# A long convolution with a gated layer on one core: the seams between its stages, and the third stage's reads in rows of 128

## The chip, the cores and the metric

The kernel runs on one core of one Trainium2 chip, in F32. Its engines are TensorE (PE; PEld is its loading of weights), VectorE (DVE), ScalarE (ACT), GpSimd (POOL) and SyncE (SP), which here only issues DMAs. DMAs are issued from SP's queue and from ACT's. The time is that of the whole program on the device in microseconds (us), the median over several runs.

## The reference

`x`, `v` are [4, 12800, 128]; the filter has an order of 64. The first half is a long causal convolution done as a product of spectra:

```python
h_mlp = np.maximum(pos_emb @ w1, 0.0) @ w2
window = np.exp(-0.01 * pos)[:, None]
h_filt = h_mlp * window
u = x * v
L = 2 * S
Uf = np.fft.rfft(u, n=L, axis=1)
Hf = np.fft.rfft(h_filt, n=L, axis=0)
y = np.fft.irfft(Uf * Hf[None, :, :], n=L, axis=1)[:, :S, :]
return (x * y).astype(np.float32)
```

Its result goes through a gated layer (`xp` is `x` with four zero rows ahead, K = 5):

```python
for k in range(K):
    gate_pre += conv_w[k][None, None, :] * xp[:, k:k + S, :]
gate = 1.0 / (1.0 + np.exp(-gate_pre))
val = x @ w_val
return (gate * val @ w_out).astype(np.float32)
```

## The kernel before, in words

The sequence of 12800 is split as J x N1 x N2 = 2 x 100 x 64. The transform of length 25600 then becomes sums over N1 and over N2, each a matmul with a table of cosines and sines. B = 4 batches and D = 128 channels make 512 columns (`BD`). The work goes in three stages, with DRAM between them.

**Stage 1** goes over 64 columns n of N2 in pairs q that mirror each other. SP reads 1 MB of `xv`, DVE multiplies x by v (L312) and forms sums and differences (`mirrored`, L321), PE multiplies by the table `fold` (L334), ACT copies the result to `st` (L336), and SP stores it to the array `a_u` in DRAM, rows 0 to 95 and 96 to 99 apart (class `_Split`, L118). The filter's work (`filt`) runs in between. Of each n there are two stores of `st`; the program's last ones are named below. While the last columns run, SP already begins to read pair 0 of the next stage: `load_pair(0, NL)` takes the first NL = 24 of 32 q. The rest comes from a second `load_a` (two DMAs, L213), whose data need the last stores.

**Stage 2** goes over 50 pairs p of rows of N1 (`NP`). `load_pair` reads 1 MB of `a_u` (and weights each fourth pair). `spectrum` multiplies by the tables (PE L419) into `z_ps`, four PSUM banks; `times` multiplies by the filter's spectrum (DVE L425) into `va`, `vb`, `vc`, `vd`; POOL adds `vb` to `va` in two parts (L504, L506) and `vd` to 768 columns of `vc` (L505); DVE adds the last 256 (L491, L494), behind a tiny copy `gate` that waits for POOL. `inverse` (PE L435) multiplies back into `c_ps` (two buffers of two banks), ACT copies that to `c_sb` (L442; two tiles, one for a pair, each for both j), and ACT's queue stores each half to the array `c_y` in DRAM (L443). The inverse of pair p - 1 stands in round p; the last round does those of 48 and 49.

```python
c_y = dram.tile([J, N1, 2 * N2, B, D], F32, name="c_y")
```

A row of `c_y` has 128 x 2 KB = 256 KB.

**Stage 3** goes over 32 groups s (`y_order`), R = 4 columns of N2 of one j in each. A group needs, for both c, 4 x 512 columns of all 100 rows of `c_y[j]`. They lie in `ag`, whose memory (the filter's spectrum in stage 1 and 2) becomes six blocks; group s takes two, so three groups fit. Groups 0 to 2 (`FIRST`) are read into it in stage 2, rows 0 to 79 by a plan (`early`), the rest when the pairs are done; later groups by `load_rows`, in halves of 1024 columns split in 96 and 4 rows: 8 DMAs a group. `load_x` reads `xr` (800 KB).

For each of the 4 columns: `y_sum` (PE L596, eight rows in the trace for two columns) multiplies 100 rows by the table `inv` into `sd`; `y_copy` (ACT L603) copies it to `sd_sb`; `y_trans` (PE L610) transposes it into `tp` and ACT copies a part to `dif` (L612); `y_join` (DVE L620, L621; POOL L623) forms y and multiplies by x, into `ext` (`tail` for a last group). Then the layer: `tap` (ACT L635, DVE L638), `sigmoid` (ACT L642), `value` (PE L647), `gated` (DVE L652), `project` (PE L657), `finish` (ACT L665 and the output's DMA from ACT's queue, L668). `WARM` matmuls on tables stand ahead of the first sums (L682).

Each stage opens pools of SBUF and PSUM (`p1`, `ps1`, `p2`, `ps2`, `p3`, `ps3`) and closes them at its end, so the next stage's tiles lie on the same memory, and the first instruction to write a tile waits for all that used that place. The loaded pairs lie in a pool `ld` of six buffers, open through stages 1 and 2. Within a stage each engine takes its instructions in the order in which they are written (`manual_schedule`); a scheduler may move those of one stage past those of another that it is not bound to. Each engine runs its own list strictly in order, so an instruction that waits holds all behind it.

Of the kernel before, what the change touches and what calls it, by code (L numbers as in the profile page):

```python
# [9 lines left out]
F32 = mybir.dt.float32  # L10
# [111 lines left out]
def tile_longconv_gate(  # L122
# [28 lines left out]
    c_y = dram.tile([J, N1, 2 * N2, B, D], F32, name="c_y")  # L151
# [3 lines left out]
    inv = const.tile([N1, 2, N2], F32, name="inv")  # L155
# [19 lines left out]
    nc.scalar.dma_start(out=inv, in_=t_inv)  # L175
# [16 lines left out]
    blocks = [ag.rearrange("p k j e -> p (k j e)")[:N1, i * CR:(i + 1) * CR] for i in range(N1 * J * FO // CR)]  # L192
# [39 lines left out]
    with tc.tile_pool(name="p1", bufs=1) as p1, tc.tile_pool(name="ps1", bufs=1, space=PSUM) as ps1:  # L232
# [112 lines left out]
        with tc.manual_schedule():  # L345
# [42 lines left out]
            store(*last)  # L388


    with tc.tile_pool(name="p2", bufs=1) as p2, tc.tile_pool(name="ps2", bufs=1, space=PSUM) as ps2:
# [37 lines left out]
        def inverse(p, j, terms):  # L429
            wk = loaded[p][1]  # L430
            c_ps = ps2.tile([128, 2, BD], F32, name="c_ps", bufs=2)
# [6 lines left out]
            if j == 0:  # L438
                c_sb = p2.tile([128, 2, J, B, D], F32, name="c_sb", bufs=2)
                outs[p] = c_sb  # L440
            c_sb = outs[p]
            nc.scalar.copy(out=c_sb[:, :, j].rearrange("p h b d -> p h (b d)"), in_=c_ps)  # L442
            nc.scalar.dma_start(  # L443
                out=c_y[j, 2 * p:2 * p + 2].rearrange("h p b d -> p h (b d)"),
                in_=c_sb[:, :, j].rearrange("p h b d -> p h (b d)"))

        outs = {}
# [11 lines left out]
        with tc.manual_schedule():  # L459
            for p in range(-1, NP + 1):  # L460
                now, nxt, old = 0 <= p < NP, p + 1 < NP, 0 <= p - 1
                if p < 0:
                    load_a(loaded[0][0], 0, NL, N2 // 2)
                for q in range(AHEAD + 1) if p < 0 else (p + AHEAD,):
                    if q < NP and q not in loaded:
                        loaded[q] = load_pair(q)
                if p in early:
# [27 lines left out]
                if now:  # L495
                    vc = p2.tile([128, 2, B, D], F32, name="vc", bufs=3)
                    vd = p2.tile([128, 2, B, D], F32, name="vd", bufs=2)
                    times(vc, z1[0], h[:, 0, 0:2], 2)
# [5 lines left out]
                    nc.gpsimd.tensor_tensor(va[:, 0:2], va[:, 0:2], vb[:, 0:2], op=ALU.add)  # L504
                    nc.gpsimd.tensor_tensor(vcf, vcf, vdf, op=ALU.add)  # L505
# [4 lines left out]
                if old:  # L510
                    if p < NP:
                        inverse(p - 1, 0, ((0, oa[:, 0]), (1, oa[:, 1])))
                    if p == NP - 1:
                        inverse(p, 0, ((0, va[:, 0]), (1, va[:, 1])))
                        for c in range(2):
                            load_k(0, c, 96, N1)
                    inverse(p - 1, 1, ((0, oa[:, 2]), (1, oa[:, 3, 0:PB]), (0, oc[:, 0]), (1, oc[:, 1])))
            for s in range(1, FIRST):
                for c in range(2):
                    load_k(s, c, 80, N1)  # L520
# [9 lines left out]
    with tc.tile_pool(name="p3", bufs=1) as p3, tc.tile_pool(name="ps3", bufs=1, space=PSUM) as ps3:  # L530
# [8 lines left out]
        def load_x(s):  # L539
# [4 lines left out]
            xr = p3.tile([D, R * ROW], F32, name="xr", bufs=2)  # L544
# [225 lines left out]
```

## Time and profile before

| | us |
|---|---|
| runs | 1163.94, 1168.69, 1157.94; median 1163.94 |
| profiled execution | 1167.67 |
| its span | 1165.5 |
| stage 1 ends, stage 2's first matmul on a loaded pair | 362.46 |
| stage 2's last store of `c_y` issued | 756.76 |
| stage 3's first copy `sd_sb` | 765.33 |

The profiled execution has 2.17 us outside its span. The span's times run from its start. In a row of a timeline stand the start, the length, the engine (with a q, its queue of DMAs), the line, what it writes and reads, and in brackets for how long the engine had been idle and who ended that. `PEclk` in a table of stretches is the share of the full clock that PE was granted; the DMA share is how busy the core's 16 DMA engines were in the mean.

### The profile page before, as it was taken

To read this page: it belongs to the slowest core of one execution; us is meant where nothing else is said; L and a number is where in the kernel's file an instruction comes from. 1 tells how busy PE (TensorE), PEld (TensorE's weight loads), DVE (VectorE), ACT (ScalarE), POOL (GpSimd) and SP (SyncE) were. 2 spreads that over 40 slices of the span, in tenths; PEclk is the share of its full clock that TensorE was granted. 3 is DMA by queue.
4 is the path that set the end of the run, shared out by engine and by line. 5 is a ranking of instruction groups with operands and counts; after the bars stand their busy time and mean duration, and the time that the engine had idled before them with its cause. 6 is when DMAs were issued, how large, how long until landed. Compare 5 with 4: busy or idle time off the path is not lost.

```text
span 1165.5 us, 17562 instructions
## 1 busy us (share of the span) xinstructions
PE 1046.1 (90%) x6208; PEld 492.1 (42%) x6208; DVE 969.3 (83%) x1150; ACT 615.7 (53%) x1000; POOL 775.2 (67%) x393
## 2 busy tenths in 40 slices
PE   4899887887764999999999999979999999999986
PEld 2455543443321444444444444434444444444432
DVE  5675445798944899999999999629999999999996
ACT  1366555665641344444444444346676767677763
POOL 3354332323313888889888889737889898898880
PEclk9999999998995899999999999988999999999999
DMA  9999999999987588988888998558999999999932
GB/s 364 350 417 403 361 352 345 353 341 350 344 268 286 209 311 300 317 300 302 303 312 287 362 339 321 178 176 218 283 288 285 264 292 278 278 289 284 284 119 113
DMA packets 92888, 344.60 MB, mean 296 GB/s; under 512 B 9774, under 2 KB 19418, under 8 KB 77610
## 3 DMA queue, kind: packets, MB, share of 16 engines
q1 hardware_dynamic: 58824, 263.74, 69.1%
q10 hardware_dynamic: 33978, 79.74, 17.8%
q8 instruction: 51, 0.84, 0.3%
q14 instruction: 35, 0.29, 0.1%
HBM read 212.37 MB, written 131.07 MB: 295 GB/s over the span
## 4 chain that ended last, share of the span: by engine, by line
PE 58%; DMA 28%; ACT 6%; DVE 4%; issue 2%; SPq 1%; ACTq 0%; DVEq 0%
PE c_ps L435 21%; DMA a_u<-st 19%; PE sd L596 9%; PE z_ps L419 9%; DMA ld<-in_xv_dram 6%; PE o_ps L657 6%; PE v_ps L647 5%; PE tp L610 5%; PE c_ps L404 2%; DVE gt L638 2%; PE fp L334 2%; ACT gt L635 1%; ACT o_sb L665 1%; DMA c_y<-c_sb 1%; ACT sg L642 1%
## 5 line engine op out<-in xcount | busy, mean ns | idle before, releaser
L623 POOL TENSOR_TENSOR ext<-yr,xr 128x400 f32<-128x400 f32 x120 | 301.6, 2515 | 44.0 <-DVE yr L621 41.9
L322 POOL TENSOR_TENSOR eo<-eo 128x512 f32<-128x512 f32 x62 | 116.8, 1904 | 212.0 <-DVE eo L321 212.0
L334 PE MATMUL fp<-eo,fold 64*128 64x512 f32 x768 | 194.4, 640 | 54.5 <-ACT st L336 40.1
L638 DVE SCALAR_TENSOR_TENSOR gt<-ext,cw,gt 128x1600 f32<-128x1600 f32 x128 | 241.5, 1887 | 0.8 <-ACT gt L635 0.8
L442 ACT COPY c_sb<-c_ps 128x1024 f32<-128x1024 f32 x100 | 101.3, 1013 | 204.6 <-PE c_ps L435 196.5
L336 ACT COPY st<-fp 128x1024 f32<-128x1024 f32 x128 | 124.2, 1015 | 133.2 <-DMA a_u<-st 81.5
L435 PE MATMUL c_ps<-va,ld 64*128 64x512 f32 (+1 forms) x800 | 166.6, 556 | 0.1
L425 DVE TENSOR_TENSOR va<-z_ps,h_sb 128x2048 f32<-128x2048 f32 x50 | 114.3, 2286 | 38.7 <-DMA ld<-a_u 30.4
L504 POOL TENSOR_TENSOR va<-va,vb 128x1024 f32<-128x1024 f32 x50 | 118.4, 2367 | 40.0 <-DVE vb L425 40.0
L419 PE MATMUL z_ps<-ld 64*64 64x512 f32 x800 | 122.4, 621 | 18.2 <-DMA ld<-a_u 16.3
L334 PEld LDWEIGHTS fp<-eo,fold 64*128 64x128 f32 x768 | 74.8, 197 | 135.8 <-issue 76.4
L596 PE MATMUL sd<-ag,inv 100*64 100x512 f32 x512 | 128.7, 620 | 1.6 <-ACT sd_sb L603 1.0
L657 PE MATMUL o_ps<-gd,wout 128*128 128x400 f32 x256 | 112.4, 521 | 19.7 <-DVE gd L652 10.9
L435 PEld LDWEIGHTS c_ps<-va,ld 64*128 64x128 f32 x800 | 74.2, 189 | 113.7 <-issue 110.2
L506 POOL TENSOR_TENSOR va<-va,vb 128x1024 f32<-128x1024 f32 x50 | 118.3, 2367 | 0.0
L603 ACT COPY sd_sb<-sd 128x512 f32<-128x512 f32 x128 | 76.1, 595 | 76.8 <-PE sd L596 54.1
L425 DVE TENSOR_TENSOR vb<-z_ps,h_sb 128x2048 f32<-128x2048 f32 x50 | 114.0, 2280 | 0.0
L647 PE MATMUL v_ps<-ext,wval 128*128 128x400 f32 x256 | 107.1, 500 | 0.0
L435 PE MATMUL c_ps<-vc,ld 64*128 64x512 f32 x400 | 94.2, 589 | 0.0
L610 PEld LDWEIGHTS tp<-ident,sd_sb 128*128 128x128 f32 x512 | 60.1, 144 | 78.9 <-PE sd L596 47.9
L505 POOL TENSOR_TENSOR vc<-vc,vd 128x768 f32<-128x768 f32 x50 | 91.2, 1824 | 2.2 <-issue 0.3
L610 PE MATMUL tp<-ident,sd_sb 128*128 128x128 f32 x512 | 81.9, 286 | 5.4 <-ACT sd_sb L603 3.8
(84 smaller groups left out, 1452.1 us busy)
## 6 DMA issues: line engine op xcount, KB each, us to landing
ld<-in_xv_dram SPq DMA_DIRECT2D x64, 1024.0 KB
c_y<-c_sb ACTq DMA_DIRECT2D x100, 512.0 KB
ld<-a_u SPq DMA_DIRECT2D x49, 1024.0 KB
a_u<-st SPq DMA_DIRECT2D x64, 768.0 KB
ag<-c_y SPq DMA_DIRECT2D x116, 384.0 KB
out_dram<-o_sb ACTq DMA_DIRECT2D x32, 800.0 KB
xr<-in_xt_dram SPq DMA_DIRECT2D x31, 800.0 KB
ld<-in_tab_w_dram SPq DMA_DIRECT2D x12, 768.0 KB
```

What stands on the lines that cost most here:

```text
L334: nc.tensor.matmul(out=fp[:, h], lhsT=fold[r, w], rhs=eo[r, o, :, l], start=i == 0, stop=i == len(terms) - 1)
L336: nc.scalar.copy(out=st[:, o].rearrange("k j (h b) d -> k h j (b d)", h=2), in_=fp)
L419: nc.tensor.matmul(out=zs[c][half[h]], lhsT=wk[half[c], 0, half[h]], rhs=a2[half[c], h, j], start=True, stop=True)
L425: nc.vector.tensor_tensor(out, z.rearrange("p (b d) -> p b d", d=D).unsqueeze(1).to_broadcast([128, n, B, D]), h_sb.unsqueeze(2).to_broadc ...
L435: nc.tensor.matmul(out=c_ps[:, h, 0:n], lhsT=wk[half[h], 1 + c], rhs=vt[half[h]].rearrange("p b d -> p (b d)"), start=(i == 0), stop=(i == ...
L504: nc.gpsimd.tensor_tensor(va[:, 0:2], va[:, 0:2], vb[:, 0:2], op=ALU.add)
L596: nc.tensor.matmul(out=sd[c * N2:(c + 1) * N2], lhsT=inv[:, c], rhs=ct[c][:, r * B * D:(r + 1) * B * D], start=True, stop=True)
L610: nc.tensor.transpose(out=tp[:, b], in_=t[:, b], identity=ident)
L623: nc.gpsimd.tensor_tensor(e[:, r0 + r], yr, xr, op=ALU.mult)
L638: nc.vector.scalar_tensor_tensor(gt, rows(t, k), cw[:, k:k + 1], gt, op0=ALU.mult, op1=ALU.add)
L647: nc.tensor.matmul(out=v_ps, lhsT=wval, rhs=rows(t)[:, r * ROW:(r + 1) * ROW], start=True, stop=True)
L657: nc.tensor.matmul(out=o_ps, lhsT=wout, rhs=gd, start=True, stop=True)
```

## The change

- The two loads of pair 0's end are written behind the last store of stage 1, not at the head of stage 2.
- `c_sb` is one tile for each inverse ([128, 2, BD], five buffers), not one for a pair (two buffers of twice the size).
- In the last pair, DVE does the addition of `va[:, 0:2]` and that of 768 columns of `vc`; POOL keeps that of `va[:, 2:4]`.
- The rows 80 to 95 of groups 0 to 2 are read ahead of the last inverses, rows 96 to 99 of all three behind the inverse (49, 0). Before, groups 1 and 2 took rows 80 to 99 at the stage's end.
- PSUM of stage 2 is in two pools, `psz` (`z_ps`) and `psc` (`c_ps`). Stage 3's first tiles (`xr`, `sd_sb`, `dif`, `yr`, `tail`; in PSUM `sd` and `tp3`) have pools of their own, `y3` and `psy`, opened ahead of `p3` and `ps3`: they come to lie on `ld` and on `z_ps`.
- Two warm-up matmuls for four, into `tp3`.
- `c_y` has J x N1 = 200 rows in one dimension. `load_rows` reads 128 of them in one DMA for each c: rows 0 to 127 for j = 0, rows 72 to 199 for j = 1 (`EDGE` = 72). In j = 1 the 100 rows needed then stand 28 lower, and `y_sum` runs over 128 rows with a table that is zero in the first 28. That table takes the place of `fold` (of which `inv` is now a view) and is read in round 4 of stage 2 from SP, 128 KB, where before 50 KB came from ACT's queue at the start.

```diff
+            load_a(loaded[0][0], 0, NL, N2 // 2)
...
-            if j == 0:
-                c_sb = p2.tile([128, 2, J, B, D], F32, name="c_sb", bufs=2)
...
+            c_sb = p2.tile([128, 2, BD], F32, name="c_sb", bufs=5)
...
-                if p < 0:
-                    load_a(loaded[0][0], 0, NL, N2 // 2)
...
+                if p == 4:
+                    nc.sync.dma_start(out=inv, in_=t_inv)
...
+                    if not nxt:
+                        nc.vector.tensor_tensor(va[:, 0:2], va[:, 0:2], vb[:, 0:2], op=ALU.add)
                     times(vc, z1[0], h[:, 0, 0:2], 2)
                     times(vd, z1[1], h[:, 1, 0:2], 2)
...
+                    else:
+                        nc.vector.tensor_tensor(vcf, vcf, vdf, op=ALU.add)
...
-            for s in range(1, FIRST):
-                for c in range(2):
-                    load_k(s, c, 80, N1)
...
+    with tc.tile_pool(name="y3", bufs=1) as y3, tc.tile_pool(name="psy", bufs=1, space=PSUM) as psy, \
+            tc.tile_pool(name="p3", bufs=1) as p3, tc.tile_pool(name="ps3", bufs=1, space=PSUM) as ps3:
...
-                rows_ = c_y[j].rearrange("k p b d -> k p (b d)")
-                for h in range(0, R, R // 2):
-                    sync_s.dma_start(
-                        out=t[:, h * B * D:(h + R // 2) * B * D],
-                        in_=rows_[:, n0 + h:n0 + h + R // 2].rearrange("k p e -> k (p e)"))
+                nc.sync.dma_start(
+                    out=t, in_=c_y[j * EDGE:j * EDGE + 128, n0:n0 + R].rearrange("k p b d -> k (p b d)"))
...
-            sd = ps3.tile([128, B * D], F32, name="sd", bufs=2)
+            k = slice(0, N1 if s < NG else 128)
+            sd = psy.tile([128, B * D], F32, name="sd", bufs=2)
...
-                    out=sd[c * N2:(c + 1) * N2], lhsT=inv[:, c], rhs=ct[c][:, r * B * D:(r + 1) * B * D],
+                    out=sd[c * N2:(c + 1) * N2], lhsT=inv[k, s // NG, c], rhs=ct[c][k, r * B * D:(r + 1) * B * D],
...
-                w_ps = ps3.tile([D, 2 * D], F32, name="o_ps", bufs=2)
-                nc.tensor.matmul(
-                    out=w_ps, lhsT=ident, rhs=dft.rearrange("p a k -> p (a k)"), start=True, stop=True)
+                w_ps = psy.tile([D, B, 128], F32, name="tp3", bufs=2)
+                nc.tensor.matmul(out=w_ps[:, 0:2], lhsT=ident, rhs=dft, start=True, stop=True)
```

How instructions move is seen in three places. First, SP's list at the end of stage 1 (`a_u<-st` are stores, `ld<-a_u` the loads of pairs; here the last two stores and the loads for pairs 0 and 1), before:

```order
L118 DMA a_u<-st 96x2048
L118 DMA a_u<-st 4x2048
L213 DMA ld<-a_u 16x2x1024
L118 DMA a_u<-st 96x2048
L118 DMA a_u<-st 4x2048
L213 DMA ld<-a_u 16x2x1024
L227 DMA ld<-a_u 128x2x1024 x3
```

and after:

```order
L121 DMA a_u<-st 96x2048
L121 DMA a_u<-st 4x2048
L121 DMA a_u<-st 96x2048
L121 DMA a_u<-st 4x2048
L215 DMA ld<-a_u 16x2x1024 x2
L229 DMA ld<-a_u 128x2x1024 x3
```

The first of the two loads stood between the last two stores; now both stand behind them.

Second, PE's list at the end of stage 2, from the last inverse of an earlier pair on (`z_ps` is `spectrum`, `c_ps` are inverses, `o_ps` and `tp_...` from `dft` the warm-up matmuls, `sd` the first sums of stage 3), before:

```order
L419 MATMUL z_ps<-ld 64x512 x8
L435 MATMUL c_ps<-va,ld 128x512 x6
L435 MATMUL c_ps<-va,ld 128x256 x2
L435 MATMUL c_ps<-vc,ld 128x512 x4
L435 MATMUL c_ps<-va,ld 128x512 x10
L435 MATMUL c_ps<-va,ld 128x256 x2
L435 MATMUL c_ps<-vc,ld 128x512 x4
L435 MATMUL c_ps<-va,ld 128x512 x2
L435 MATMUL c_ps<-va,ld 128x256 x2
L435 MATMUL c_ps<-vc,ld 128x512 x4
L682 MATMUL o_ps<-dft,ident 128x256 x4
L596 MATMUL sd<-ag,inv 64x512 x4
```

and after:

```order
L423 MATMUL z_ps<-ld 64x512 x8
L439 MATMUL c_ps<-va,ld 128x512 x6
L439 MATMUL c_ps<-va,ld 128x256 x2
L439 MATMUL c_ps<-vc,ld 128x512 x4
L684 MATMUL tp_5505<-dft,ident 128x256
L684 MATMUL tp_5507<-dft,ident 128x256
L439 MATMUL c_ps<-va,ld 128x512 x10
L439 MATMUL c_ps<-va,ld 128x256 x2
L439 MATMUL c_ps<-vc,ld 128x512 x4
L439 MATMUL c_ps<-va,ld 128x512 x2
L439 MATMUL c_ps<-va,ld 128x256 x2
L439 MATMUL c_ps<-vc,ld 128x512 x4
```

The warm-up matmuls now stand ahead of the inverses of pairs 48 and 49, and the sums follow the last inverse directly. The banks of `tp` are those of `z_ps`.

Third, DVE's list at the same place (`va`, `vb`, `vc`, `vd` of pair 49 come from `z_ps` and the filter's spectrum `h_sb`; `gate` and the rows beside it belong to pair 48 or 49's inverse), before:

```order
L425 TENSOR_TENSOR va<-z_ps,h_sb_5264 128x2048
L425 TENSOR_TENSOR vb<-z_ps,h_sb_5264 128x2048
L491 TENSOR_TENSOR vc<-vc,vd 128x256
L493 COPY gate<-va 128x1
L494 TENSOR_TENSOR vc<-vc,va 128x256
L425 TENSOR_TENSOR vc<-z_ps,h_sb_5264 128x1024
L425 TENSOR_TENSOR vd<-z_ps,h_sb_5264 128x1024
```

and after:

```order
L429 TENSOR_TENSOR va<-z_ps,h_sb_5312 128x2048
L429 TENSOR_TENSOR vb<-z_ps,h_sb_5312 128x2048
L490 TENSOR_TENSOR vc<-vc,vd 128x256
L492 COPY gate<-va 128x1
L493 TENSOR_TENSOR vc<-vc,va 128x256
L498 TENSOR_TENSOR va<-va,vb 128x1024
L429 TENSOR_TENSOR vc<-z_ps,h_sb_5312 128x1024
L429 TENSOR_TENSOR vd<-z_ps,h_sb_5312 128x1024
L509 TENSOR_TENSOR vc<-vc,vd 128x768
```

The addition L498 stands ahead of the last two products that read `z_ps`, and L509 right behind them.

More of the change, by code (lines that the diff above doesn't have):

```diff
@@ L29 @@
 R = 4
-WARM = 4
+WARM = 2
 NC1 = N1 // 2 + 1
+EDGE = J * N1 - 128
 def _tables():
@@ L149, in tile_longconv_gate @@
     a_u = dram.tile([N1, 2, N2 // 2, 2, J, B, D], F32, name="a_u")
-    c_y = dram.tile([J, N1, 2 * N2, B, D], F32, name="c_y")
+    c_y = dram.tile([J * N1, 2 * N2, B, D], F32, name="c_y")
     fwd = const.tile([N1, 3, N1], F32, name="fwd")
     fold = const.tile([128, 3, 128], F32, name="fold")
-    inv = const.tile([N1, 2, N2], F32, name="inv")
+    inv = fold[:, 0:2].rearrange("p j (c n) -> p j c n", c=2)
     win = const.tile([N1, J, N2], F32, name="win")
@@ L191, in tile_longconv_gate @@
     CR = R * B * D
-    blocks = [ag.rearrange("p k j e -> p (k j e)")[:N1, i * CR:(i + 1) * CR] for i in range(N1 * J * FO // CR)]
+    blocks = [ag.rearrange("p k j e -> p (k j e)")[:, i * CR:(i + 1) * CR] for i in range(N1 * J * FO // CR)]
     y_order = [(j, g) for j in range(J) for g in [N2 // R - 1] + list(range(N2 // R - 1))]
@@ L202, in load_k @@
         nc.sync.dma_start(
-            out=block(s, c)[k0:k1], in_=c_y[j, k0:k1, n0:n0 + R].rearrange("k p b d -> k (p b d)"))
+            out=block(s, c)[k0:k1], in_=c_y[j * N1 + k0:j * N1 + k1, n0:n0 + R].rearrange("k p b d -> k (p b d)"))
     NP, PG = N1 // 2, KG // 2
@@ L388, in tile_longconv_gate @@
             store(*last)
-    with tc.tile_pool(name="p2", bufs=1) as p2, tc.tile_pool(name="ps2", bufs=1, space=PSUM) as ps2:
+            load_a(loaded[0][0], 0, NL, N2 // 2)
+    with tc.tile_pool(name="p2", bufs=1) as p2, tc.tile_pool(name="psz", bufs=1, space=PSUM) as psz, \
+            tc.tile_pool(name="psc", bufs=1, space=PSUM) as psc:
         BD = B * D
@@ L395, in bank @@
         def bank():
-            return ps2.tile([128, BD], F32, name="z_ps", bufs=4)
+            return psz.tile([128, BD], F32, name="z_ps", bufs=4)
         def filter_pair(p):
-            h_ps = ps2.tile([128, J, BD], F32, name="c_ps", bufs=2)[:, :, 0:2 * D].rearrange("p j (c d) -> p j c d", c=2)
+            h_ps = psc.tile([128, J, BD], F32, name="c_ps", bufs=2)[:, :, 0:2 * D].rearrange("p j (c d) -> p j c d", c=2)
             for c in range(2):
@@ L430, in inverse @@
             wk = loaded[p][1]
-            c_ps = ps2.tile([128, 2, BD], F32, name="c_ps", bufs=2)
+            c_ps = psc.tile([128, 2, BD], F32, name="c_ps", bufs=2)
             for i, (c, vt) in enumerate(terms):
@@ L437, in inverse @@
                         start=(i == 0), stop=(i == len(terms) - 1))
-            if j == 0:
-                c_sb = p2.tile([128, 2, J, B, D], F32, name="c_sb", bufs=2)
[L440 to L447, printed above, removed]
+            c_sb = p2.tile([128, 2, BD], F32, name="c_sb", bufs=5)
+            nc.scalar.copy(out=c_sb, in_=c_ps)
+            nc.scalar.dma_start(out=c_y[j * N1 + 2 * p:j * N1 + 2 * p + 2].rearrange("h p b d -> p h (b d)"), in_=c_sb)
         filt_p, z_p, v_p = {}, {}, {}
@@ L473, in tile_longconv_gate @@
                 if p == NP - 1:
-                    for c in range(2):
-                        load_k(0, c, 80, 96)
+                    for s in range(FIRST):
+                        for c in range(2):
+                            load_k(s, c, 80, 96)
                 if now:
@@ L514, in tile_longconv_gate @@
                         inverse(p, 0, ((0, va[:, 0]), (1, va[:, 1])))
[L515 to L516 removed]
+                        for s in range(FIRST):
+                            for c in range(2):
+                                load_k(s, c, 96, N1)
                     inverse(p - 1, 1, ((0, oa[:, 2]), (1, oa[:, 3, 0:PB]), (0, oc[:, 0]), (1, oc[:, 1])))
[L518 to L520 removed]
     ld_pool.__exit__(None, None, None)
[L530 removed]
+    with tc.tile_pool(name="y3", bufs=1) as y3, tc.tile_pool(name="psy", bufs=1, space=PSUM) as psy, \
+            tc.tile_pool(name="p3", bufs=1) as p3, tc.tile_pool(name="ps3", bufs=1, space=PSUM) as ps3:
         HALO = KC - 1
@@ L601, in y_copy @@
         def y_copy(s, r):
-            t = p3.tile([128, B, D], F32, name="sd_sb", bufs=3)
+            t = y3.tile([128, B, D], F32, name="sd_sb", bufs=3)
             nc.scalar.copy(out=t.rearrange("p b d -> p (b d)"), in_=sds.pop((s, r)))
```

23 lines of the change are left out of this document (12 added, 11 removed).

## The prediction

> **What bounds the kernel now.** I read the page first: the span and the share of each engine.
>
> ```profile
> span 1165.5 us, 17562 instructions
> PE 1046.1 (90%) x6208; PEld 492.1 (42%) x6208; DVE 969.3 (83%) x1150; ACT 615.7 (53%) x1000; POOL 775.2 (67%) x393
> ```
>
> TensorE (PE) is busy 90% of the span, so there are some 119 us in which it is not. The next view is the busy time by stretches, which shows where they lie.
>
> ```profile
> core 0: us, PE busy (x) PEld busy (x) DVE busy (x) ACT busy (x) POOL busy (x), PEclk, DMA share, GB/s
> 330.00:375.00 45.00, 23.53 (x150) 9.52 (x148) 14.41 (x11) 13.75 (x21) 5.73 (x3) 0.74 0.80 265
> 400.00:500.00 100.00, 100.00 (x738) 44.21 (x736) 98.54 (x92) 41.80 (x66) 90.34 (x53) 1.00 0.85 297
> 740.00:760.00 20.00, 18.21 (x88) 8.53 (x82) 8.04 (x10) 6.08 (x6) 11.11 (x6) 1.00 0.63 200
> 760.00:780.00 20.00, 16.16 (x68) 6.68 (x68) 3.87 (x13) 7.57 (x17) 6.17 (x6) 0.83 0.67 199
> 780.00:800.00 20.00, 17.25 (x72) 7.35 (x71) 15.57 (x21) 12.09 (x22) 12.82 (x8) 0.83 0.68 192
> 900.00:1000.00 100.00, 96.99 (x410) 44.54 (x409) 96.28 (x137) 72.45 (x128) 88.75 (x35) 1.00 0.94 280
> ```
>
> Stage 2 (400 to 500) and stage 3 (900 to 1000) leave PE nothing or 3%; in stage 3 VectorE (DVE) has as little room, and the DMA engines stand at 0.94. PE idles at the seams: 21 us from 330 to 375, some 8 from 740 to 800, and in both the granted clock drops. The change works on both seams and on stage 3's transfers, so there are three terms: A, B and C.
>
> **A: the first pair's end of load, put last in stage 1.** SyncE's (SP's) timeline, the chain of waits and PE's timeline at the first seam:
>
> ```profile
> 343.66 11.24 DMA a_u<-st
> 354.92 0.32 SPq L213 DMA_DIRECT2D ld<-a_u  x1
> 355.33 0.74 SPq L118 DMA_DIRECT2D a_u<-st  x2
> 359.60 0.32 SPq L213 DMA_DIRECT2D ld<-a_u  x1
> 362.46 3.54 PE L419 MATMUL z_ps<-ld 64*64 64x512 f32 x16 [16.29 <-DMA ld<-a_u]
> ```
>
> The first half of the load (L213) goes out at 354.92, when the last store but one has landed (343.66 + 11.24 = 354.90). The last store stands behind it on SP and goes at 355.33; the second half waits for that, goes at 359.60, and PE starts 2.86 us later. After the change both halves stand behind the last store, which then follows the other without the 10 us of waiting. If the two overlap, the last store lands soon after 354.9. From its own issue it needed 359.60 - 355.33 = 4.27 us, some of which is its bytes queued behind its predecessor's; I let it land 2 us after, at 357.0. The load goes then, 2.6 us earlier. Bounds: 0 (all 4.27 us follow the predecessor) and 4.3 (they vanish in its 11.24). PE is full from 400 on, so nothing is late behind it: **A = -2.6**.
>
> **B: the seam from stage 2 to 3.** The timelines of ScalarE (ACT), PE, and DVE:
>
> ```profile
> 751.25 1.01 ACT L442 COPY c_sb<-c_ps 128x1024 f32<-128x1024 f32 x1 [2.87 <-DMA c_y<-c_sb]
> 765.33 1.07 ACT L603 COPY sd_sb<-sd 128x512 f32<-128x512 f32 x2 [8.59 <-DMA c_y<-c_sb]
> ```
>
> ```profile
> 745.43 5.12 PE L435 MATMUL c_ps<-va,ld 64*128 64x512 f32 x24
> 753.77 1.91 PE L435 MATMUL c_ps<-vc,ld 64*128 64x512 f32 x8
> 756.79 1.99 PE L682 MATMUL o_ps<-dft,ident 128*128 128x256 f32 x8 [1.10 <-ACT c_sb L442]
> 759.33 2.79 PE L596 MATMUL sd<-ag,inv 100*64 100x512 f32 x8 [0.55 <-DMA ag<-c_y]
> 765.97 1.11 PE L610 MATMUL tp<-ident,sd_sb 128*128 128x128 f32 x4 [3.85 <-ACT sd_sb L603]
> 767.08 3.61 PE sd L596 x8
> ```
>
> ```profile
> 744.78 1.22 DVE L425 TENSOR_TENSOR vc<-z_ps,h_sb 128x1024 f32<-128x1024 f32 x1
> 745.91 1.22 DVE L425 TENSOR_TENSOR vd<-z_ps,h_sb 128x1024 f32<-128x1024 f32 x1
> L321 DVE TENSOR_TENSOR eo<-u,ld 128x1024 f32<-128x1024 f32 x64 | 76.9, 1240 | 4.8 <-PE fp L334 0.9
> ```
>
> Stage 3's first copy waits 8.59 us, to 765.33, for the last c_y store: its tile lies on memory that the store still reads. With pools of their own the copy waits for the sums and its PSUM bank only. That would be worth all of 765.33 - 759 less a sum, were PE not delayed first. It is: the order shows the two warm-up matmuls ahead of the last two pairs' inverses, in `psy`, on the banks that DVE's last `vd` reads. In before `vd` ends at 745.91 + 1.22 = 747.13. Ahead of it now stands an addition of 1024 columns that GpSimd (POOL) did; the nearest row is L321's, 1.24 us. So `vd` ends at 748.3. PE, which in before began its next matmuls at 745.43, waits 2.9 us with the four inverses queued behind. Then two warm-ups (half of 1.99): 749.3. The inverses took from 745.43 to 753.77 + 1.91 = 755.68, 10.25 us: they end at 759.5. Pair 49's first store follows the second inverse, at about a third of the four's 10.25 us, so 752.8, and its copy of 1.01: it goes at 753.9, where before it went at 752.3 (the copy of 751.25 was that one). Its landing and the small read of its rows bring the sums some 1.6 us later than before's 759.33 less the two warm-ups' time saved: I take 759.6, and 760.6 for the first copy. Gain 4.7 us.
>
> Behind the copy, before's sums ran slowly: 3.61 us for eight, against 1.87 in the rows below, a stretch at half clock. If it goes, 2.8 us more are won (1.74 on these eight, the rest on the transposes and sums beside them): B = -7.5. If PE's new wait of 2.9 us brings a throttled stretch of its own, as waits do between 760 and 800 (clock 0.83 with PE busy 81 to 86%, hence 0.17 x 20 = 3.4 us lost in each), little of the 2.8 stays and up to 2.7 more go: -2. I take **B = -6.0**, nearer to the first.
>
> [...]
>
> **C: stage 3's reads of c_y.** The chain of waits gives the period of a step (8 steps from the first of these rows to the last), SP's timeline the issue, the page the sizes:
>
> ```profile
> 804.75 1.87 PE sd L596 x8
> 862.35 1.87 PE sd L596 x8
> 897.30 1.87 PE sd L596 x8
> 842.42 5.19 SPq L118 DMA_DIRECT2D ag<-c_y  x8
> ag<-c_y SPq DMA_DIRECT2D x116, 384.0 KB
> ag<-c_y SPq DMA_DIRECT2D x116, 16.0 KB
> xr<-in_xt_dram SPq DMA_DIRECT2D x31, 800.0 KB
> out_dram<-o_sb ACTq DMA_DIRECT2D x32, 800.0 KB
> ```
>
> A step takes (897.30 - 804.75) / 8 = 11.57 us. It reads 4 x (384 + 16) = 1600 KB of c_y in 29 steps. Now it reads 2 x 1024 = 2048 KB, 28% more, in 2 DMAs for 8. The price hangs on the rate; these answers show the transfers while one kind runs nearly alone: c_y in rows of 8 KB (628, 714.9), in 4 KB (787.5), `xr` (768), the output (852).
>
> ```profile
> DMA packets 61, 0.50 MB, mean 250 GB/s; under 512 B 0, under 2 KB 0, under 8 KB 0
> DMA packets 54, 0.43 MB, mean 266 GB/s; under 512 B 2, under 2 KB 2, under 8 KB 2
> DMA packets 318, 1.09 MB, mean 242 GB/s; under 512 B 54, under 2 KB 54, under 8 KB 316
> DMA packets 150, 0.86 MB, mean 429 GB/s; under 512 B 16, under 2 KB 16, under 8 KB 150
> DMA packets 110, 0.59 MB, mean 397 GB/s; under 512 B 12, under 2 KB 12, under 8 KB 110
> ```
>
> c_y comes at 242 to 266 GB/s, `xr` and the output at 429 and 397. Transfers of one step: `xr` 0.819 / 0.429 = 1.91, output 0.819 / 0.397 = 2.06, c_y 2.097 MB at 258 (the middle of the 8 KB rows) 8.13: 12.1 us. Against 11.57 the DMA engines become the bound, by 0.53 x 29 = 15.4 us; from this goes what the buffers hold: a read issued at 842.42 is used at 862.35, 19.9 us later, and needs about one period, so 8.6 are slack. That leaves 6.8. [...] Bounds: at 266 GB/s 11.85 us, 8.1 us in all, within the slack, so 0; at 242 it is 12.64, 31 - 8.6 = +22.
>
> [...]
>
> **At nothing**, with what covers it: the fold table's 128 KB read in pair 4 on SP (ACT loses a read at the start; stage 2 has a DMA share of 0.85); K = 128 in place of 100 (a matmul's time goes with its columns: 620 ns at K = 100 and 621 at 64 in the groups); five `c_sb` (ACT is busy 41.8 of 100, only the wait of 2.87 at the seam counts, and it is in B); last-pair additions (POOL has less to do, DVE's 1.2 us are in B). The groups for K:
>
> ```profile
> L596 PE MATMUL sd<-ag,inv 100*64 100x512 f32 x512 | 128.7, 620 | 1.6 <-ACT sd_sb L603 1.0
> L419 PE MATMUL z_ps<-ld 64*64 64x512 f32 x800 | 122.4, 621 | 18.2 <-DMA ld<-a_u 16.3
> ```
>
> Sum: -2.6 - 6.0 + 4 = -4.6. The profiled execution took 1167.67 (2.2 outside its span), 3.7 over the median 1163.94; taken off the median: **1159**.
>
> **Rivals.** First, slower: stage 3 becomes bound by its transfers. From 0.6 us over the period on, thus below 256 GB/s, C eats A and B; at 242, +22 gives 1163.94 + 13.4 = 1177, at 250 (12.36 us, +14.3) 1170. For it speak the DMA share of 0.94 before a byte is added, and the slowest of the c_y rows; against it that PE there never waits for a read. [...] Second, B is lost: warm-ups ahead of the inverses, PE waiting behind `vd`, a slow clock behind that. B = -2, in all -0.6: 1163. Third, all gains: whole rows over all partitions reach 266 or more, the clock stays up, A lies between its middle and its bound: -10.1 to -11.8, so 1152 to 1154. Fourth, the load's new place does nothing, since the last store's bytes follow the other's anyway: A = 0, 1162; it lies within the others.
>
> **Chances.** Forecast 0.45 (A and B as worked out, C from 0 to 9: 1155 to 1164), slow reads 0.25, B lost 0.1, all gains 0.2. A measurement of this kernel can't tell less than 1% (11.6 us) from no change. Faster by more than that, under 1152.3, is the better half of all gains, 0.1, and 0.08 that I add to either side for what no row shows: 0.18. Slower, over 1175.6, needs C of 20, reads at 244 or less: half of the slow reads, 0.12, and the same 0.08: 0.2. The rest, 0.62, lies within. The range goes from the better end of all gains with the unknown's first part, 1148, to slow reads at 242, 1177.
>
> **What would show it.** A: the load on SP issued at about 357 and PE's first `z_ps` at 359.9. B: a gap of PE of 2.9 us ahead of the warm-ups, released by DVE's `vd`; the first `sd_sb` copy right behind the first sums, with no wait for a c_y store; the clock between 760 and 800 at 0.9 or above. C: stage 3's period, 11.57 or longer, PE's sums waiting for `ag` or not, the DMA share near 1.0 and over 300 GB/s. The prediction is wrong if the sums wait for reads by more than 18 us in all, or if stage 1 or 2 takes another time between its seams.

## The result, and the profile after

| | before | changed |
|---|---|---|
| median, first comparison (9 runs each) | 1163.94 | 1155.03 |
| ratio, with its 95% interval | | 0.9917 (0.9891 to 0.9944) |
| median, second comparison (33 and 12 runs) | 1163.31 | 1157.37 |
| ratio, with its 95% interval | | 0.9948 (0.9919 to 0.9976) |
| span of the profiled execution | 1165.5 | 1155.8 |

The change makes the kernel faster by some 6 to 9 us, under 1%; both intervals lie below 1. The forecast was 1159, with "within 1%" as the likeliest case. A ratio is estimated by itself and differs a little from the quotient of the medians (1155.03 / 1163.94 would be 0.9923). Three executions fell in a slower state, one of before (beside the first four variants), one of the changed kernel with the old reads and the profiled one of the run that reads rows 80 to 91 earlier, so the medians below leave them out and that profile's times aren't compared.

The page of the changed kernel begins so, and its table of stretches (the columns are those of before's) follows.

```profile
span 1155.8 us, 17291 instructions
PE 1045.2 (90%) x6204; PEld 488.4 (42%) x6204; DVE 963.2 (83%) x1152; ACT 616.3 (53%) x1000; POOL 775.2 (67%) x391
```

```profile
330.00:375.00 45.00, 28.51 (x156) 9.77 (x156) 19.88 (x17) 10.43 (x18) 14.07 (x9) 0.68 0.80 270
740.00:760.00 20.00, 17.62 (x60) 6.72 (x59) 0.56 (x3) 4.75 (x6) 0.00 (x0) 0.76 0.74 152
760.00:780.00 20.00, 18.24 (x92) 7.75 (x91) 8.00 (x22) 12.48 (x27) 10.22 (x10) 0.94 0.68 249
780.00:800.00 20.00, 17.65 (x75) 8.38 (x74) 20.00 (x29) 12.41 (x20) 18.18 (x7) 0.91 0.67 257
900.00:1000.00 100.00, 97.00 (x412) 44.40 (x408) 96.29 (x137) 72.16 (x125) 88.56 (x35) 1.00 0.81 314
```

PE's busy time is the same to 1 us, so what was won is waiting. Two things stand out. The clock is now lower than before between 740 and 760 (0.76 against 1.00), ahead of the place where it was low, and higher behind it (0.94 and 0.91 from 760 to 800, against 0.83 twice). And stage 3 (900 to 1000) moves 314 GB/s against 280, more as its reads are longer, with a *smaller* share of DMA time: 0.81 against 0.94.

The first seam, in the chain of waits, SP's timeline and PE's timeline:

```profile
338.70 11.51 DMA a_u<-st
348.13 2.47 SPq L215 DMA_DIRECT2D ld<-a_u  x2
353.01 3.46 PE L423 MATMUL z_ps<-ld 64*64 64x512 f32 x16 [13.17 <-DMA ld<-a_u]
```

The last store goes at 338.70, when its copy is done, and not 10 us later. The load's two halves wait for the last two stores: the first goes at 348.13, when the last store but one has landed, the second at 350.3, when the last has (338.70 + 11.51 = 350.21). So the last store lands 2.1 us after the other.

The second seam, in DVE's, PE's and ACT's timelines and the chain of waits:

```profile
737.56 1.21 DVE L429 TENSOR_TENSOR vd<-z_ps,h_sb 128x1024 f32<-128x1024 f32 x1
738.92 2.04 PE L684 MATMUL tp<-dft,ident 128*128 128x256 f32 x4 [2.82 <-DVE vd L429]
740.89 7.12 PE L439 MATMUL c_ps<-va,ld 64*128 64x512 f32 x24
753.52 1.04 PE L598 MATMUL sd<-ag,fold 100*64 100x512 f32 x2 [0.79 <-DMA ag<-c_y]
756.16 3.68 PE L598 MATMUL sd<-ag,fold 100*64 100x512 f32 x6 [1.60 <-DMA ag<-c_y]
758.17 0.58 ACT L605 COPY sd_sb<-sd 128x512 f32<-128x512 f32 x1 [4.37 <-PE sd L598]
```

```profile
747.82 2.96 DMA c_y<-c_sb
751.13 4.99 DMA ag<-c_y
```

The copy into `sd_sb` no longer waits for a store. The hoisted warm-ups wait 2.82 us for DVE's `vd`. Behind them 24 matmuls of the inverses take 7.12 us, where 24 took 5.12 in before: the granted clock is 0.50 from 738.39 to 745.22. Pair 49's store goes at 747.82. The first two of the eight rows of sums run at 753.52; the other six need another read of rows 96 to 99, which goes at 751.13 and takes 4.99 us.

Stage 3, by the chain of waits and by the transfers from 791 to 794, where c_y is read almost alone:

```profile
794.87 1.87 PE sd L598 x8
887.42 1.87 PE sd L598 x8
DMA packets 171, 1.27 MB, mean 423 GB/s; under 512 B 16, under 2 KB 16, under 8 KB 16
```

Between the same two groups as in before lie (887.42 - 794.87) / 8 = 11.57 us a step, unchanged. The reads run at 423 GB/s, where before's ran at 242 to 268.

### The profile page after: what moved, and what is told of

It reads as the page before. It is cut to its first block, busy times and chain, and to the rows that moved or that the text cites. A ratio compares the mean times of both kernels' runs of the same rounds, so it can differ in the third digit from the quotient of the medians.

```text
span 1155.8 us, 17291 instructions
## 1 busy us (share of the span) xinstructions
PE 1045.2 (90%) x6204; PEld 488.4 (42%) x6204; DVE 963.2 (83%) x1152; ACT 616.3 (53%) x1000; POOL 775.2 (67%) x391
## 4 chain that ended last, share of the span: by engine, by line
PE 59%; DMA 25%; DVE 7%; ACT 6%; issue 2%; ACTq 0%; POOL 0%; SPq 0%; DVEq 0%
PE c_ps L439 20%; DMA a_u<-st 13%; PE sd L598 9%; DMA ld<-in_xv_dram 9%; PE z_ps L423 9%; PE o_ps L659 6%; PE v_ps L649 5%; PE tp L612 5%; PE fp L336 2%; PE c_ps L408 2%; DVE gt L640 2%; DMA ld<-in_pos_dram 2%; ACT gt L637 1%; ACT o_sb L667 1%; DVE va L429 1%
## 5 line engine op out<-in xcount | busy, mean ns | idle before, releaser
L598 PE MATMUL sd<-ag,fold 100*64 100x512 f32 (+1 forms) x512 | 128.2, 616 | 3.4 <-DMA ag<-c_y 2.4
L659 PE MATMUL o_ps<-gd,wout 128*128 128x400 f32 x256 | 112.3, 520 | 17.8 <-DVE gd L654 9.0
```

The source lines that it names most:

```text
L598: nc.tensor.matmul(out=sd[c * N2:(c + 1) * N2], lhsT=inv[k, s // NG, c], rhs=ct[c][k, r * B * D:(r + 1) * B * D], start=True, stop=True)
L659: nc.tensor.matmul(out=o_ps, lhsT=wout, rhs=gd, start=True, stop=True)
```

## The experiments

The question was which part of the change brought the gain, and where. The profiled executions are split at three marks: the last copy into `st`, stage 2's first `z_ps` on a loaded pair, and stage 3's first `sd_sb` copy. The changed kernel's last copy into `st` starts 6.3 us earlier than before's:

```profile
344.00 1.01 ACT L336 COPY st<-fp 128x1024 f32<-128x1024 f32 x1 [0.72 <-PE fp L334]
```

```profile
337.67 1.01 ACT L338 COPY st<-fp 128x1024 f32<-128x1024 f32 x1 [0.72 <-PE fp L336]
```

That lies ahead of the seam, and no step of the prediction speaks of it.

### The table's read moved alone

```diff
-    nc.scalar.dma_start(out=inv, in_=t_inv)
...
+                if p == 4:
+                    nc.sync.dma_start(out=inv, in_=t_inv)
```

> The kernel before with one edit: the table `inv` is read in round 4 of stage 2 from SP, not from ACT's queue at the start. In the changed kernel's profile the last copy into `st` ends stage 1 6.3 us earlier than in before (337.67 against 344.00), and the lead begins with ACT's first copy (18.65 against 20.32). Theory T (the table's read held ACT's first copies by a place in the queue, and stage 1 keeps and enlarges that lead): last `st` copy at 336 to 340, the time 4 to 7 us under before. Theory N (the lead beyond 1.7 us is chance of one execution): the last `st` copy may fall anywhere from 337 to 345, and the time is 0 to 2 us under before.

Measured: 1162.14 against 1163.41, ratio 0.9997 (0.9968 to 1.0025). The last `st` copy starts at 344.42. ACT's first copy does come 1.9 us earlier (19.67, by the same mark 21.61 in before), but nothing of this is left at the stage's end. Theory T falls.

### The load's place alone

```diff
-                if p < 0:
-                    load_a(loaded[0][0], 0, NL, N2 // 2)
...
             store(*last)
+            load_a(loaded[0][0], 0, NL, N2 // 2)
```

> The kernel before with one edit: the two loads of pair 0's end stand behind the last store. Theory A as forecast: from the last copy into `st` to stage 2's first matmul on the load 2.6 us less than before's 18.5 (362.46 - 344.00), so 15.9, and the time 2 to 4 us under before. Rival: the last store's bytes follow its predecessor's anyway, the distance stays at 18 and the time within 1 us of before.

Measured: 1160.81 against 1163.41, ratio 0.9996 (0.9969 to 1.0024). In its profile, ACT's last copy into `st` and PE's first `z_ps`:

```profile
340.47 1.01 ACT L336 COPY st<-fp 128x1024 f32<-128x1024 f32 x1 [0.72 <-PE fp L334]
355.34 3.69 PE L420 MATMUL z_ps<-ld 64*64 64x512 f32 x16 [12.71 <-DMA ld<-a_u]
```

From the one to the other are 14.9 us, 3.6 less than before's 18.5. The full kernels without the move in this study show 17.4 to 18.5 (before and three more), those with it 14.1 to 15.4 (five; 16.6 in the run that reads rows 80 to 91 earlier, left out here): the means lie 3.0 us apart. The step is there; the timed ratio, 0.5 us under before where 2 to 4 were expected, couldn't have shown it, since its interval is 6 us wide.

### The changed kernel with the old reads

```diff
-                nc.sync.dma_start(
-                    out=t, in_=c_y[j * EDGE:j * EDGE + 128, n0:n0 + R].rearrange("k p b d -> k (p b d)"))
+                rows_ = c_y[j * N1:(j + 1) * N1].rearrange("k p b d -> k p (b d)")
+                for h in range(0, R, R // 2):
+                    sync_s.dma_start(
+                        out=t[:N1, h * B * D:(h + R // 2) * B * D],
+                        in_=rows_[:, n0 + h:n0 + h + R // 2].rearrange("k p e -> k (p e)"))
```

> The changed kernel with before's reads of c_y in stage 3 (100 rows in halves, 96 and 4 rows, 8 DMAs a group, K = 100). Theory C as forecast (the longer reads cost 0 to 9 us): this kernel 0 to 9 us faster than the changed one, stage 3's period 11.57 us. Theory D (the reads are hidden, since the changed kernel's DMA share in stage 3 fell from 0.94 to 0.81): within 1.5 us of the changed kernel, with a DMA share back at 0.94. Theory E (128 rows are what won): 3 us or more slower.

Measured: 1158.19 (1158.77 with the execution that is left out), ratio 0.9971 (0.9935 to 1.0007), so 3.2 us over the changed kernel's median of the first comparison and 0.8 over that of the second; the intervals overlap. In its profile stage 3 has the DMA share back at 0.93 and the period as before. It speaks for D, and can't exclude E. This kernel and the load's place alone, measured together, differ by B's edits and the table: 0.9971 against 0.9996, 2.9 us, the intervals overlapping. No run comes nearer to B by itself.

### The changed kernel without warm-up

```diff
-WARM = 2
+WARM = 0
```

> The changed kernel without its two warm-up matmuls. In its profile they wait 2.8 us for DVE's `vd`, take 2.0 and leave PE at half clock through the four inverses (the first of them 3.8 us, 1.7 in before). Theory W (that wait and the throttle behind it ate B): the first `sd_sb` copy 4 to 7 us nearer to DVE's last `vd` than in the changed kernel (758.17 - 737.56 = 20.6), so 14 to 17 us, and the time 3 to 6 us under the changed kernel. Rival (the reads of rows 96 to 99 set the seam, landing 5 us after their issue whatever PE does): the distance 19 to 20.6 and the time within 1.5 us.

Measured: 1152.2, ratio 0.9923 (0.9889 to 0.9956). From DVE's last `vd` to the first copy are now 16.2 us for 20.6, inside what theory W expected; but PE waits elsewhere:

```profile
748.68 4.53 PE L598 MATMUL sd<-ag,fold 100*64 100x512 f32 x8 [5.04 <-DMA ag<-c_y]
```

The inverses are done at 743.6 and PE idles for 5.04 us until the last rows have come; then the first eight sums take 4.53 us, the next eight 1.94. The ratio can't be told from the changed kernel's. From stage 2's first `z_ps` to the first `sd_sb` copy it takes 399.9 us, where the three profiles with the warm-ups take 403.6 to 405.2. Both theories have a part: the warm-ups' wait goes, and the reads set the seam.

### The changed kernel once more, the table alone, the table and the reads

> The changed kernel itself once more, beside the others of this call on one chip. What is asked of its profile is stage 1: in the profiles so far the last copy into `st` starts at 337.67 (changed), 336.10 and 337.24 (its two variants), against 344.00 (before), 344.42 and 340.47 (variants of before), and the data rate from 30 to 180 us is 391, 391 and 392 GB/s against 375, 378 and 385. Theory P (a real effect of the change on stage 1): again 335 to 339 and 390 GB/s or more. Theory N (chance): anywhere from 335 to 345.

Measured: 1157.37, ratio 0.9948 (0.9919 to 0.9976). The last `st` copy starts at 340.13, the data rate from 30 to 180 us is 383 GB/s. Both are outside what theory P asked for.

The next takes the new table alone; the edit to the sum is

```diff
-                    out=sd[c * N2:(c + 1) * N2], lhsT=inv[:, c], rhs=ct[c][:, r * B * D:(r + 1) * B * D],
+                    out=sd[c * N2:(c + 1) * N2], lhsT=inv[:N1, 0, c], rhs=ct[c][:, r * B * D:(r + 1) * B * D],
```

beside `inv = fold[:, 0:2]...`, its longer table and the read in round 4, as in the change.

> The kernel before with the new table alone: `inv` is a view of `fold`, its table has [128, 2, 2, 64] elements (128 KB for 50 KB) and is read in round 4 from SP; stage 3 uses the first 100 rows of j = 0's. Against the run with the read moved alone, this takes 512 bytes of every partition out of the constants ahead of stage 1's tiles and lengthens an input in DRAM. Theory P (places of tiles or arrays quicken stage 1's transfers): the last `st` copy at 335 to 339, 390 GB/s from 30 to 180, the time 4 to 6 us under before. Theory N: 340 to 345 and within 2 us of before.

Measured: 1161.87, ratio 0.999 (0.9961 to 1.0018); the last `st` copy at 345.79, 378 GB/s. Stage 1's instructions and the places of its tiles are the changed kernel's here, up to the load's place, and yet this is the latest end of stage 1 of all. Theory P falls: what separates 336 from 346 is not this part of the change.

Then the table with the reads of 128 rows (`c_y` in 200 rows, `EDGE`, `load_rows` and `y_sum` as in the change; the rest as in before):

> The kernel before with the new table and the reads of 128 rows, 2 DMAs a group in stage 3, K = 128 for j = 1; everything else as before. Against the run with the table alone it shows the price of the reads. Theory C as forecast: 0 to 9 us slower than that run. Theory D (hidden): within 1.5 us, stage 3 from its first copy to the end as in before (400.2 us from the first `sd_sb` copy at 765.33 to the span's end at 1165.5). Theory E (the reads win, as the changed kernel with the old reads suggests, 1158.8 against 1155.0): stage 3 1 to 4 us shorter.

Measured: 1159.39, ratio 0.9971 (0.9946 to 0.9996), 2.5 us under the run with the table alone, their intervals overlapping. The stretch from 900 to 1000 of the two, the table alone first:

```profile
900.00:1000.00 100.00, 96.99 (x411) 44.41 (x408) 96.28 (x137) 70.10 (x128) 88.69 (x35) 1.00 0.95 278
```

```profile
900.00:1000.00 100.00, 96.98 (x410) 44.41 (x408) 96.28 (x137) 70.79 (x124) 88.56 (x35) 1.00 0.81 314
```

PE and DVE are busy to 0.01 us the same, the DMA share falls from 0.95 to 0.81. The reads cost nothing here, since they are faster; and they bring nothing, since PE and DVE set the step. The length from the first `sd_sb` copy to the end can't decide between D and E: it is 397.4 us with the table alone, 399.5 with the reads and 400.2 in before, and the five profiles of before and its variants scatter by 3 us.

### Rows 80 to 91 read earlier

```diff
+                if p == NP - 3:
+                    for s in range(FIRST):
+                        for c in range(2):
+                            load_k(s, c, 80, 92)
                 if p == NP - 1:
...
-                            load_k(s, c, 80, 96)
+                            load_k(s, c, 92, 96)
```

> The changed kernel without warm-up, and with rows 80 to 91 of groups 0 to 2 read in round 47, so that only rows 92 to 95 are left for round 49. In the run without warm-up PE is done with the inverses at 743.6 and waits 5.0 us for rows 96 to 99: pair 49's store went at 738.72 and landed 6.8 us later, among the reads of rows 80 to 95 (0.8 MB). If these are what delays it: it lands 2 to 3 us earlier, PE's wait is 2 to 3 us, and the time is 2 to 4 us under the run without warm-up. If the stores themselves (0.5 MB each, four behind one another) set it: no change within 1 us.

Measured: 1154.49 (1154.85 with the execution that is left out), ratio 0.9917 (0.9885 to 0.9948), against 1157.37 for the changed kernel measured beside it; the intervals overlap, so it isn't shown to be better. Against the run without warm-up (0.9923) it is 0.7 us less by the ratios, where 2 to 4 were expected if the early reads were to help. PE's wait ahead of the first sums hasn't gone from its profile: PE stands idle for 6.6 us there, with no releaser shown.

### Four kernels with a quiet stage 1

The single times of each kernel so far spread over some 11 us or more, and their ratios leave effects of 3 us open. The profiles showed most of the scatter in stage 1, which is bound by transfers up to 330 us (in before the DMA share is 0.99 from 30 to 180 us, 0.97 from 180 to 330). So stage 1's reads were cut in four kernels:

```diff
-            nc.sync.dma_start(out=t, in_=xv[n_seq[i]].rearrange("h q w j l b d -> (h q) (w j l b d)"))
+            if i < XB:
+              nc.sync.dma_start(out=t, in_=xv[n_seq[i]].rearrange("h q w j l b d -> (h q) (w j l b d)"))
```

> The kernel before, with 59 of stage 1's 64 reads of `xv` left out (their products are taken of the first five tiles again, so the result is another; every other instruction stays). The profiles so far put nearly all scatter into stage 1, whose last `st` copy lies between 336 and 346 us without a pattern. Without the reads stage 1 waits less for DMA and should scatter less: single times within 4 us, where they now spread over 12 or more. This run is the measure for the next three. If the times spread as before, the scatter is in the stores to `a_u`, and the four say little.

> The changed kernel with the same reads left out. Against the quiet before: forecast -4.6 us (A -2.6, B -6.0, C +4). From the segments of the ten profiles so far: A -2.7, the seam +1 to +2, stage 3 0 to -1, in all -1 to -3 us. If the measured -6 to -9 us of the full kernels are in the seams and stage 3: -6 to -9.

> The changed kernel with before's reads of c_y, the same reads of `xv` left out. Theory D (the reads of 128 rows are hidden): within 1 us of the quiet changed kernel. Theory E (they win, as two timed pairs suggest, 2 to 4 us): 2 to 4 us slower than that. Theory C (they cost): up to 9 us faster.

> The changed kernel without its two warm-up matmuls, the same reads of `xv` left out. Theory W: 3 to 6 us under the quiet changed kernel, since the wait of 2.8 us behind `vd`, the warm-ups' 2.0 us and the half clock behind them go. Rival: within 1.5 us, since the last rows' reads set the seam.

| quiet kernel | median | lowest to highest |
|---|---|---|
| before | 1120.03 | 1119.16 to 1122.27 |
| changed | 1114.68 | 1113.87 to 1121.68 |
| changed, old reads | 1114.90 | 1113.20 to 1117.41 |
| changed, no warm-up | 1114.27 | 1113.31 to 1118.47 |

The changed kernel is 5.35 us faster by the medians (1120.03 - 1114.68) and 4.5 by the means (1120.61 - 1116.14), near the forecast's 4.6 and under what the full kernels show; one of its six times lies among before's. The old reads make 0.2 us, the warm-ups 0.4: neither can be told from nothing. That speaks for D. Theory W's 3 to 6 us are not there; but the half clock behind the wait, which W counts on, is missing from the quiet profiles with the warm-ups (24 matmuls of the inverses take 4.99 and 5.00 us there, 7.12 in the changed kernel), so they don't try W for the full kernel.

The marks of the two quiet profiles, before first (ACT's last `st` copy, PE's first `z_ps`, the store of pair 49's first half, PE's first sums, ACT's first `sd_sb` copy):

```profile
span 1120.1 us, 17419 instructions
301.61 1.01 ACT L337 COPY st<-fp 128x1024 f32<-128x1024 f32 x1 [0.72 <-PE fp L335]
318.00 3.80 PE L420 MATMUL z_ps<-ld 64*64 64x512 f32 x16 [14.21 <-DMA ld<-a_u]
706.85 0.37 ACTq L444 DMA_DIRECT2D c_y<-c_sb  x1
713.57 3.12 PE L597 MATMUL sd<-ag,inv 100*64 100x512 f32 x8
720.20 1.07 ACT L604 COPY sd_sb<-sd 128x512 f32<-128x512 f32 x2 [8.61 <-DMA c_y<-c_sb]
```

And changed, with the warm-ups and the inverses behind them:

```profile
span 1115.6 us, 17150 instructions
304.02 1.01 ACT L339 COPY st<-fp 128x1024 f32<-128x1024 f32 x1 [0.72 <-PE fp L337]
317.73 3.69 PE L424 MATMUL z_ps<-ld 64*64 64x512 f32 x16 [11.55 <-DMA ld<-a_u]
702.58 1.10 PE L685 MATMUL tp<-dft,ident 128*128 128x256 f32 x4 [2.80 <-DVE vd L430]
703.61 4.99 PE L440 MATMUL c_ps<-va,ld 64*128 64x512 f32 x24
708.40 0.37 ACTq L445 DMA_DIRECT2D c_y<-c_sb  x1
715.97 4.00 PE L599 MATMUL sd<-ag,fold 100*64 100x512 f32 x8 [2.64 <-DMA ag<-c_y]
718.30 0.59 ACT L606 COPY sd_sb<-sd 128x512 f32<-128x512 f32 x1 [3.92 <-PE sd L599]
```

The spans of the four profiles, cut at the marks:

| stretch | before | changed | difference | quiet before | quiet changed | difference |
|---|---|---|---|---|---|---|
| start to last `st` copy | 344.0 | 337.7 | -6.3 | 301.6 | 304.0 | +2.4 |
| to first `z_ps` (A) | 18.5 | 15.3 | -3.1 | 16.4 | 13.7 | -2.7 |
| to first `sd_sb` copy (B) | 402.9 | 405.2 | +2.3 | 402.2 | 400.6 | -1.6 |
| to the end (B's clock, and C) | 400.2 | 397.6 | -2.6 | 399.9 | 397.3 | -2.6 |
| span | 1165.5 | 1155.8 | -9.7 | 1120.1 | 1115.6 | -4.5 |

The largest single difference of the full pair, 6.3 us in stage 1, is the one that no part of the change has been found to make. The other three make -3.4 in the full pair and -6.9 in the quiet one. Between these two the difference is in the third row.

One pair is a thin base where single stretches scatter by several us. All profiles, but the one left out (ranges, with the mean behind):

| profiles | start to last `st` copy | to first `z_ps` | from there to the end |
|---|---|---|---|
| before, table's read moved, table alone, table and reads | 338.9 to 345.8, 343.3 | 17.4 to 18.5, 17.8 | 798.4 to 803.1, 801.2 |
| load's place alone | 340.5 | 14.9 | 800.0 |
| changed (two), changed with the old reads | 336.1 to 340.1, 338.0 | 14.1 to 15.4, 14.9 | 801.6 to 802.8, 802.2 |
| changed, no warm-up | 337.2 | 14.7 | 796.0 |
| quiet before | 301.6 | 16.4 | 802.1 |
| quiet changed, with old reads, without warm-up | 299.1 to 304.0, 301.4 | 13.5 to 13.7, 13.6 | 797.5 to 798.3, 797.9 |

By the means of the first and third rows the full kernel's profiles become 7.3 us shorter: 5.3 in stage 1 and 2.9 in A, while the seam to stage 3 and stage 3 together (B and C) take 1.0 longer. In the quiet kernels B and C together bring 4.2.

Without the warm-ups, PE in the quiet kernel waits 5.8 us for the last rows in place of 2.80 + 2.64:

```profile
712.67 4.49 PE L599 MATMUL sd<-ag,fold 100*64 100x512 f32 x8 [5.76 <-DMA ag<-c_y]
```

A wait taken away ahead of the inverses came back behind them; in the full kernel without warm-up 3.7 to 5.2 us stay won up to the first copy.

## Why the prediction was right, and where it wasn't

The time and the sign came out: 1155 and 1157 for 1159, inside the range. The terms did so less evenly. One sign that the prediction named for being wrong also showed: stage 1 takes "another time between its seams", 6.3 us less in the first pair.

**A, forecast -2.6: right.** It was -3.1 in the full pair and -2.7 in the quiet one, and -3.0 between the means of the full profiles. Its working held in its parts too: the last store lands 2.1 us behind its predecessor, where 2 were taken.

**B, forecast -6.0: right in mechanism, mis-sized.** The wait of the first copy for the store is gone, and by the pairs shown the slow stretch behind it mostly too (the -2.6 of the last row, where 2.8 were forecast; the five profiles of before and its variants scatter by 3.1 us in this row, so in the full kernel it isn't shown). PE's wait behind `vd` was there, 2.82 us for 2.9. The step that failed is "its landing and the small read of its rows bring the sums ... I take 759.6, and 760.6 for the first copy", a gain of 4.7 us. The quiet pair shows it piece by piece, from stage 2's first `z_ps` on. Pair 49's store goes 1.8 us later (706.85 - 318.00 = 388.9 in before, 708.40 - 317.73 = 390.7 in the changed kernel), where 1.6 were forecast. From the store to the first sums it takes 7.6 us (708.40 to 715.97), 6.7 in before (706.85 to 713.57); the forecast had 5.7 (753.9 to 759.6), less than the 7.0 that before's own profile shows (752.3 to 759.33). From the first sums to the copy it takes 2.3 us, where 1.0 were forecast, since the sums run slowly (4.00 us for eight) after PE's wait for the rows. So the copy came 1.6 us earlier, not 4.7.

In the full kernel the first sums start 5.7 us behind the store, as forecast (747.82 to 753.52), but the rest of them only after 8.3 (756.16): 2.96 for the store's landing and 4.99 for the read of rows 96 to 99 that they wait for. In the full kernel the second rival's mechanism took back more than the 1.6: after the same wait of 2.8 us the inverses ran slow (24 matmuls in 7.12 us against 4.99 in the quiet kernel, 2.1 us, and 0.9 more on the warm-ups ahead of them). That rival had a chance of 0.1, and a B of -2; the full pair shows -0.3 (+2.3 - 2.6), and the means of the profiles +1.0 for B and C. So in the full kernel the step "I take B = -6.0, nearer to the first" failed too. The wait's price depends on something besides its length; the same 2.8 us brought the slow stretch in all three full profiles that have the warm-ups ahead of the inverses, and in neither of the two quiet ones.

The record of the granted clock shows what it is. In each profile the stretches of half clock begin whole multiples of 3.41 us apart and last whole multiples of it, but for one that the end cuts off (in the changed kernel's from 738.39 for 6.83, from 755.46 for 6.83, from 786.18 for 3.41; in before's from 764.96 and 788.85 for 6.83 each), so each profiled execution has a grid of such windows, with a place of its own. These are the windows over which the wait of 2.8 us lies:

| profile | window, us from the span's start | PE busy in it, of 3.41 us | clock in the next window |
|---|---|---|---|
| changed | 734.98 to 738.39 | 1.12 | 0.50 |
| changed once more | 737.08 to 740.49 | 1.27 | 0.50 |
| changed, old reads | 731.58 to 734.99 | 1.38 | 0.50 |
| quiet changed | 697.55 to 700.96 | 2.23 | 1.00 |
| quiet changed | 700.96 to 704.37 | 1.79 | 1.00 |
| quiet changed, old reads | 693.32 to 696.73 | 1.82 | 1.00 |
| quiet changed, old reads | 696.73 to 700.14 | 2.20 | 1.00 |

In the three full profiles most of the wait fell into one window; in the two quiet ones a border between windows cut it in two. From 400 to 1100 us of the profiles of before and changed, five windows at full clock were followed by one at half clock; PE was busy in them for 0.57, 1.12, 1.57, 1.73 and 2.00 us, and for 2.02 us or more in all others. The quiet rows with 1.79 and 1.82 us had full clock behind them, so PE's busy time in one window doesn't decide it alone. By these profiles, whether this wait costs 3 us or nothing is in part the luck of an execution, and the quiet kernels' better third row is partly that.

**C, forecast +4: wrong, it is 0 as far as the runs can tell.** The failed step is the rate: "c_y 2.097 MB at 258 (the middle of the 8 KB rows)". It runs at 423. The rows I took were of c_y, of the right length, but over 64 and 80 partitions. The row that would have served was `xr`'s, also over 128 partitions, at 429, and it stood in the same fence. By it a step's transfers are 1.91 + 2.06 + 2.097 / 0.423 = 8.9 us, well under 11.57. Rival one, slow reads at 0.25, had the same mistake in it. No run shows the +4 of the sum, and the 2.8 us between it and the 6.8 of the working had no row behind them. In the runs the period stayed at 11.57 us, and with the old reads the quiet kernel's median was 0.2 us off.

For rows of 8 KB the traces have 250 GB/s over 64 partitions, 266 over 80 and 423 over 128. Whether the partitions alone make this, and whether they also explain the old reads' 242 to 268 over 96, stays open, since those have rows of 4 KB; no run changed the partitions and the row's length one at a time.

**What hid the errors:** in the quiet kernel B gave 1.8 us less than forecast (-4.2 for -6.0) and C cost 4 us less; so the forecast sum of -4.6 stands near the measured -5.35 in part because two errors have opposite signs. In the full kernel's profiles B and C together bring nothing, A brings 3 us, and 5 us come from a stage that no term speaks of. That the full kernel's time hit the forecast is in good part luck.

**What stays open:** the full kernel's gain of 6 to 9 us against the -3.4 of its profile's own seams. In stage 1 the last copy came at 336.1, 337.2, 337.7 and 340.1 in four profiles of the changed family, at 342.2 in a fifth (the run that reads rows 80 to 91 earlier), and at 338.9 to 345.8 in five of before's. Moving the table's read, the table and its place were each tried and don't make that; stage 1's own instructions are otherwise the same. Ten profiles with a scatter of 10 us don't settle whether it is chance. The timed runs also had a slightly higher mean clock in the changed kernel (0.977 and 0.975, against 0.972), which would fit seams that are throttled less often there than in the one profile shown; that is argued, not shown. B's edits were not run by themselves, neither together nor the last pair's additions and `c_sb` singly.

## What to carry to other kernels

Price a transfer by a row of the trace that covers the same partitions, not only by one of the same array and row length (here 423 GB/s over 128 partitions, 250 and 266 over 64 and 80). When a wait is taken off a seam, follow the chain one step further, here from the store to the small read of its rows: if the same data must land anyway, a wait removed early returns late, in whole or in part (without the warm-ups 5.76 us for 2.80 + 2.64 in the quiet kernel). Look at the clock over several executions before pricing a wait of PE's: the same 2.8 us cost some 3 us more or nothing. And where the scatter of one stage hides what is asked of another, quiet that stage and compare again; 5 us in 1120 could then be read from five or six executions.

## What the runs showed of the hardware

Reading 128 rows of 8 KB, 256 KB apart, ran at 423 GB/s, and the old reads in 96 and 4 rows at 242 to 268, so 28% more bytes took less of the DMA engines' time (0.81 for 0.94). A wait of PE of 2.8 us in otherwise full work was followed by half clock in three profiles and by none in two. Half clock came in whole windows of 3.41 us, on a grid that lies elsewhere in each profile; from 400 to 1100 us of before and changed it followed five windows with PE busy for 0.57 to 2.00 us of them, and none with 2.02 or more. Stage 1, bound by transfers (DMA share 0.99 and 0.97 in before), ended anywhere from 336 to 346 us with the same instructions up to its last load; cutting its reads brought the spread of single times from some 11 us or more to 3 to 8.
